# Where a ScalarE step of a weight conversion stands, the order of the second layer's products, and how far they trail, in an mLSTM, mixture-of-experts and MLP kernel on one core

## The chip, the cores and the metric

One core of a Trainium2 chip runs the whole program. Its engines work through instruction queues of their own, each in program order: TensorE (PE; its weight loads are shown apart as PEld), VectorE (DVE), ScalarE (ACT), GpSimd (POOL) and SyncE (SP), which only starts transfers here. The metric is the device time of one execution in microseconds (us), the median of several runs.

## The reference

Three stages follow each other. The middle one and the last matter here:

```python
x = attn_out.transpose(0, 2, 1, 3).reshape(B * S, H * D)   # mLSTM recurrence, 3072 tokens x 320
# mixture of experts: each token goes to the one expert (of 8) with the largest cosine
for e in range(E):
    mask = expert_idx == e
    h = np.maximum(x[mask] @ w1[e], 0.0)                    # 320 -> 1024
    out[mask] = gate_w[mask, None] * (h @ w2[e])            # 1024 -> 320
# gated MLP on all tokens
h = x @ w_in                                                # 320 -> 2048
g = h * (1.0 / (1.0 + np.exp(-1.702 * h)))
return (g @ w_out).astype(np.float32)                       # 2048 -> 320
```

The MLP's two weight arrays are float64; everything else is float32.

## The kernel before

**Stages.** The recurrence and the routing take the first part of the execution, and no edited line runs there. Then come 8 expert blocks (the loop over `steps`, 8 steps of 128 hidden units each), four of them 512 tokens wide, four 384. Then 7 MLP blocks, numbered 8 to 14, of 16 steps each: five 512 tokens wide, two 256.

**Split numbers.** Every float32 operand is kept as a high part and a remainder, so a product takes three matmuls: high by high, high by low, low by high. In a step, `h_mm` makes one PSUM tile `hp` from 8 matmuls (L138). Then the activation is split: for an expert, ACT makes the high part `hh` (L1093), and DVE the low part `hl` from it (L1094); for an MLP block the chain is `sg` on ACT (L1104), product on DVE (L1105), high part on ACT (L1106), low part on DVE (L1107). Then `o_mm` (L1120) adds three products for each of up to four 128-token row tiles into the PSUM tiles `acc`. In the last step of a block `o_mm` takes row tile after row tile with all three products (the `sorted` branch); in the others it makes all first products, then all second, then all with the low part.

**Trailing.** `o_mm` of a step stands in PE's queue after `h_mm` of a later step: one step later for the experts; for the MLP, two steps later in block 8 and in the two small blocks, one step later in blocks 9 to 12 (the list `left`). `put` and `put_out` copy `acc` to `o` after a block's last `o_mm`.

**Weights.** In each expert step ACT also casts the high parts of coming expert weights (L105, L118), and POOL (L110) and DVE (L111, L121) make their low parts. The float64 weights of the MLP are converted piece by piece meanwhile, 32 pieces, by the generator `cvt`: each `next` issues one stage of a piece, and `convert(n)` issues n stages at the end of a step (2 or 3 in wide blocks, 1 or 2 in narrow ones, 2 in block 8). First stage: ACT makes the fraction `fr` (L1160), DVE takes out the exponent `ex` (L1161), ACT turns it into `es` (L1163). The stages behind are DVE's: `mt` (L1165), `fr` (L1167), `es` (L1169, which reads ACT's `es`), `fr` (L1171). What is put on the list `late` is issued at the start of the next call of `convert`; before the change only the cast of a finished piece is put there.

The order in all queues is the order in which this code is written out (`manual_schedule`), and tile pools decide which buffer is reused.

Of the kernel before, what the change touches and what calls it, by code (L numbers as in the profile page):

```python
# [13 lines left out]
AF = mybir.ActivationFunctionType  # L14
# [6 lines left out]
CAP = 512  # L21
# [5 lines left out]
def kernel(ctx, tc, qT_in, kT_in, kvo_in, i_gate, f_gate, expert_emb, tau, w12, wio, out, dbg=None):  # L27

    nc = tc.nc
# [3 lines left out]
    E = expert_emb.shape[0]  # L33
# [972 lines left out]
    with ExitStack() as mctx:  # L1006
# [35 lines left out]
        ncol = lambda blk: GN if blk == "g" else COLS[blk]  # L1042
# [37 lines left out]
        def h_mm(blk, key, w, c0=0):  # L1080
            hp = ps_h.tile([P, CAP], F32, tag="hp", name="hp")
            nb = ncol(blk)
            hp_t[key] = hp[:, c0:nb]
            h_seq(hp_t[key], w, xh_t[blk][:, :, c0:nb], xl_t[blk][:, :, c0:nb])
# [12 lines left out]
        def swish_split(key):  # L1097
            hp = hp_t.pop(key)
            nb = hp.shape[-1]
            t = ring.tile([P, 2, CAP], F32, tag="w", name="sg")  # L1100
            sg, g = t[:, 0, 0:nb], t[:, 1, 0:nb]
            t = ring.tile([P, 2, CAP], F32R, tag="w", name="hhl")
            hh, hl = t[:, 0, 0:nb], t[:, 1, 0:nb]
            nc.scalar.activation(out=sg, in_=hp, func=AF.Sigmoid, scale=1.702)  # L1104
            nc.vector.tensor_tensor(out=g, in0=hp, in1=sg, op=ALU.mult)  # L1105
            nc.scalar.copy(hh, g)  # L1106
            nc.vector.tensor_tensor(out=hl, in0=g, in1=hh.bitcast(F32), op=ALU.subtract)  # L1107
            hs_t[key] = halves(hh, hl)

        def o_mm(blk, key, w, first, last):  # L1110
            hs = hs_t.pop(key)
            if first:
                acc_t[blk] = [ps_a.tile([P, DM], F32, tag="acc", name="acc") for _ in range(ncol(blk) // P)]


            n = ncol(blk) // P
            order_ = [(i, j) for j in range(3) for i in range(n)]
            for i, j in sorted(order_) if last else order_:
                hh, hl = hs[i]
                nc.tensor.matmul(acc_t[blk][i], hl if j == 2 else hh, w[:, DM:2 * DM] if j == 1 else w[:, 0:DM],  # L1120
                                 start=(first and j == 0), stop=(last and j == 2))
# [28 lines left out]
        exb = mp1.tile([P, 1], F32, name="exb")  # L1150

        def cvt(src, n, then):

            lo, hi = src[:, :, 0], src[:, :, 1]
            ex = mp2.tile([P, n], I32, tag="ex", name="ex", bufs=1)
            es = mp2.tile([P, n], I32, tag="sb", name="es", bufs=1)
            mt = mp2.tile([P, n], I32, tag="mt", name="mt", bufs=1)
            fr = mp2.tile([P, n], F32, tag="fr", name="fr")

            nc.scalar.activation(out=fr, in_=lo.bitcast(U32), func=AF.Copy, scale=2.0 ** -52, bias=1.0)  # L1160
            nc.vector.tensor_scalar(out=ex, in0=hi, scalar1=20, scalar2=0x7ff, op0=ALU.logical_shift_right, op1=ALU.bitwise_and)  # L1161

            nc.scalar.activation(out=es, in_=ex, func=AF.Relu, scale=float(2 ** 23), bias=exb)  # L1163
            yield
            nc.vector.tensor_scalar(out=mt, in0=hi, scalar1=0xfffff, scalar2=None, op0=ALU.bitwise_and)  # L1165
            yield
            nc.vector.scalar_tensor_tensor(out=fr, in0=mt, scalar=2.0 ** -20, in1=fr, op0=ALU.mult, op1=ALU.add)  # L1167
            yield
            nc.vector.scalar_tensor_tensor(out=es, in0=hi, scalar=-2147483648, in1=es, op0=ALU.bitwise_and, op1=ALU.bitwise_or)  # L1169
            yield  # L1170
            nc.vector.tensor_tensor(out=fr, in0=fr, in1=es.bitcast(F32), op=ALU.mult)  # L1171
            late.append(lambda: then(fr))
            yield

        craw, late = {}, []
# [6 lines left out]
        def cvt_all():  # L1182
            for m in range(M2):
                if 0 < m < M2 - 1:
                    load_c(m + 1)
                t = craw.pop(m)
                yield from cvt(t[:, 0:3 * P], 3 * P, lambda r, m=m: split_w1(win[:, m], r.rearrange("p (c f) -> p c f", c=3)))
                yield from cvt(t[:, 3 * P:], DM, lambda r, m=m: split_w2(wout[:, m], r))
# [49 lines left out]
        def load_y(blk):  # L1238
            n = ncol(blk)
            xg = xp.tile([P, NB, 3 * P], F32, tag="xr", name="xr", bufs=1)[:, 0:n // P]  # L1240
            src = y[row0(blk):row0(blk) + n, :].rearrange("(i p) d -> p i d", p=P)
            nc.sync.dma_start(out=xg[:, :, 0:DM], in_=src)
            nc.sync.dma_start(out=xg[:, :, DM:3 * P], in_=src[:, :, 2 * P:DM])
            xr_t[blk] = xg

        def scale_y(blk, eng=nc.gpsimd):
            n, t0 = ncol(blk) // P, row0(blk) // P
            eng.tensor_tensor(out=xr_t[blk], in0=xr_t[blk], in1=gated[:, t0:t0 + n].unsqueeze(2).to_broadcast([P, n, 3 * P]),  # L1248
                                    op=ALU.mult)
# [14 lines left out]
        def planes(blk, j, i):  # L1264

            if i == 0:
                xp_t[blk, j] = [half_tile(U16).rearrange("p (a i d) -> p a i d", a=2, d=3 * P),
                                half_tile(U16).rearrange("p (a c t) -> p a c t", a=2, t=GH)]
            pl, xT = xp_t[blk, j]
            nc.vector.tensor_copy(pl[:, :, i], xr_t[blk][:, j * GH // P + i].bitcast(U16).rearrange("p (d a) -> p a d", a=2))  # L1270
            for a in range(2):
                nc.sync.dma_start_transpose(out=xT[:, a, :, i * P:(i + 1) * P], in_=pl[:, a, i])

        def words(blk, j, a):

            if a == 0:
                xp_t[blk, j].append(half_tile(U16))
            pl, xT, t = xp_t[blk, j]
            nc.vector.tensor_copy(t.rearrange("p (n a) -> p a n", a=2)[:, a], xT[:, a].rearrange("p c t -> p (c t)"))

        def parts(blk, j, c):
            x = xp_t[blk, j][2].bitcast(F32).rearrange("p (c t) -> p c t", c=3)[:, c]
            if j == 0 and c == 0:
                xh_t[blk] = mp2.tile([P, 3, CAP], F32R, tag="xh", name="xh")
                xl_t[blk] = mp2.tile([P, 3, CAP], F32R, tag="xl", name="xl")
            js = slice(j * GH, (j + 1) * GH)
            nc.scalar.copy(xh_t[blk][:, c, js], x)  # L1287
            nc.vector.tensor_tensor(out=xl_t[blk][:, c, js], in0=x, in1=xh_t[blk][:, c, js].bitcast(F32), op=ALU.subtract)  # L1288
# [92 lines left out]
        with tc.manual_schedule():  # L1381
# [23 lines left out]
            def convert(n):  # L1405

                now, late[:] = late[:], []
                for f in now:
                    f()
                for _ in range(n):  # L1410
                    next(conv, None)

            def tail(p):
                e, m, s = p
                o_mm(e, ("a", s), wslot.pop(s)[1], m == 0, m == M1 - 1)
                if m == M1 - 1:
                    put(e)
# [55 lines left out]
            left = [prev]  # L1473
            for blk in range(E, len(COLS)):
                for m in range(M2):
                    h_mm(blk, ("b", blk, m), win[:, m])
                    swish_split(("b", blk, m))
                    left.append((blk, m))

                    while len(left) > (1 if E < blk and ncol(blk) == CAP else 2):  # L1480
                        p = left.pop(0)
                        (tail2 if len(p) == 2 else tail)(p)
                    if blk == E:
                        convert(2)
                    nxt = blk + 1
                    if nxt < len(COLS):
                        t = m - (2 if blk == E else 0)
                        small = ncol(blk) < CAP
                        if t == 2:
                            scale_y(nxt, nc.vector if small else nc.gpsimd)  # L1490
                        for j in range(ncol(nxt) // GH):
                            t0 = t - 3 * j
                            if 3 <= t0 < 5:
                                planes(nxt, j, t0 - 3)
                            w0 = t0 - (8 if small else 6)
                            if 0 <= w0 < 2:
                                words(nxt, j, w0)
                            if 2 <= w0 < 5:
                                parts(nxt, j, w0 - 2)
                        if t == 8 and nxt + 1 < len(COLS):  # L1500
                            load_y(nxt + 1)
# [68 lines left out]
```

## Time and profile before

| | |
|---|---|
| median of 3 runs | 806.28 us (805.17 to 807.76) |
| the profiled execution | 812.62 us, of which 810.9 us are the span |
| PE busy | 754.5 us (93%) |
| DVE busy | 566.7 us (70%) |
| ACT busy | 352.7 us (43%) |
| POOL busy | 250.9 us (31%) |

Times in the profile run from the first instruction. "Busy" is time in which an engine has at least one instruction in work; an idle gap in front of an instruction is given with the engine, operation and tile that ended it.

### The profile page before, as it was taken

To read this page: it belongs to the slowest core of one execution; us is meant where nothing else is said; L and a number is where in the kernel's file an instruction comes from. 1 tells how busy PE (TensorE), PEld (TensorE's weight loads), DVE (VectorE), ACT (ScalarE), POOL (GpSimd) and SP (SyncE) were. 2 spreads that over 40 slices of the span, in tenths; PEclk is the share of its full clock that TensorE was granted. 3 is DMA by queue.
4 is the path that set the end of the run, shared out by engine and by line. 5 is a ranking of instruction groups with operands and counts; after the bars stand their busy time and mean duration, and the time that the engine had idled before them with its cause. 6 is when DMAs were issued, how large, how long until landed. Compare 5 with 4: busy or idle time off the path is not lost.

```text
span 810.9 us, 13161 instructions
## 1 busy us (share of the span) xinstructions
PE 754.5 (93%) x4708; PEld 695.7 (86%) x4708; DVE 566.7 (70%) x1146; ACT 352.7 (43%) x834; POOL 250.9 (31%) x362
## 2 busy tenths in 40 slices
PE   6899898899799999999899999999999999999995
PEld 6899898898788788888889887888889898889995
DVE  8878888997498988888896777554454454445542
ACT  4352423324455555566564444333333343334442
POOL 5653567785132433345430100300300300201011
PEclk9788988989899999999999999999999999999998
DMA  7977866752636637557634212120120110200100
GB/s 207 321 240 248 270 204 217 243 188 94 210 117 200 224 110 236 146 176 198 194 106 144 90 20 59 38 53 20 46 66 1 53 40 1 71 1 17 38 17 16
DMA packets 70303, 100.20 MB, mean 124 GB/s; under 512 B 31120, under 2 KB 56472, under 8 KB 70232
## 3 DMA queue, kind: packets, MB, share of 16 engines
q1 hardware_dynamic: 67160, 91.41, 36.7%
q0 software_dynamic: 3072, 7.89, 2.6%
q8 instruction: 38, 0.62, 0.3%
q14 instruction: 33, 0.27, 0.1%
HBM read 77.53 MB, written 17.82 MB: 118 GB/s over the span
## 4 chain that ended last, share of the span: by engine, by line
issue 36%; DVE 12%; PE 5%; POOL 4%; ACT 4%; POOLq 0%; DVEq 0%; ACTq 0%
POOL out_dram L1142 3%; PE acc L1120 3%; PE hp L138 2%; DVE w L121 2%; DVE w L111 1%; POOL xr L1248 1%; DVE es L1169 1%; DVE fr L1167 1%; DVE hl L1094 1%; ACT hh L1093 1%; DVE sg L1105 1%; DVE ex L1161 1%; ACT hhl L1106 1%; DVE fr L1171 1%; DVE hhl L1107 1%
## 5 line engine op out<-in xcount | busy, mean ns | idle before, releaser
L1120 PE MATMUL acc<-wout,hhl 128*128 128x320 f32 x1152 | 187.8, 310 | 1.3 <-DVE hhl L1107 1.0
L1120 PEld LDWEIGHTS acc<-wout,hhl 128*128 128x128 f32 x1152 | 175.9, 188 | 9.6 <-DVE hhl L1107 1.2
L138 PE MATMUL hp<-xh,win 128*128 128x512 f32 (+1 forms) x560 | 131.5, 364 | 2.2 <-ACT xh L1287 1.5
L1105 DVE TENSOR_TENSOR sg<-hp,sg 128x512 f32<-128x512 f32 (+1 forms) x112 | 68.8, 614 | 88.5 <-ACT sg L1104 83.6
L1107 DVE TENSOR_TENSOR hhl<-sg,hhl 128x512 fp32r<-128x512 f32 (+1 forms) x112 | 73.4, 656 | 70.0 <-ACT hhl L1106 69.1
L1104 ACT ACTIVATE sg<-hp 128x512 f32<-128x512 f32 (+1 forms) x112 | 60.0, 536 | 113.2 <-PE hp L138 111.3
L1142 POOL DMA_INDIRECT out_dram<-o,tokd x24 | 23.7, 988 | 275.4 <-ACT o L1129 271.8
L138 PEld LDWEIGHTS hp<-xh,win 128*128 128x128 f32 x560 | 93.8, 188 | 14.5 <-ACT xh L1287 2.0
L1106 ACT CAST hhl<-sg 128x512 fp32r<-128x512 f32 (+1 forms) x112 | 62.6, 559 | 89.4 <-DVE sg L1105 85.8
L1120 PE MATMUL acc<-w,hh 128*128 128x320 f32 x424 | 81.0, 316 | 6.4 <-ACT hh L1093 5.2
L110 POOL TENSOR_TENSOR w<-r,w 128x256 fp32r<-128x256 f32 x58 | 45.8, 790 | 129.1 <-ACT w L105 126.6
L138 PE MATMUL hp<-xl,win 128*128 128x512 f32 (+1 forms) x336 | 85.7, 363 | 0.0
L1120 PEld LDWEIGHTS acc<-w,hh 128*128 128x128 f32 x424 | 67.2, 188 | 16.1 <-ACT hh L1093 10.6
L138 PE MATMUL hp<-xh,w 128*128 128x384 f32 (+2 forms) x320 | 75.8, 368 | 0.0
L138 PEld LDWEIGHTS hp<-xl,win 128*128 128x128 f32 x336 | 58.8, 189 | 11.0 <-DVE xl L1288 0.2
L400 PE MATMUL sp<-qT,kblk 120*128 120x128 f32 x384 | 58.1, 315 | 2.6 <-DVE wm L405 2.6
L360 DVE TENSOR_TENSOR_SCAN pm<-fb,ident_h 128x1024 f32<-128x1024 f32 x23 | 56.8, 2469 | 3.6 <-DMA fb<-dec 3.6
L138 PEld LDWEIGHTS hp<-xh,w 128*128 128x128 f32 x320 | 55.1, 193 | 3.7
L400 PEld LDWEIGHTS sp<-qT,kblk 120*128 120x128 f32 x384 | 54.6, 226 | 3.3 <-DVE wm L405 2.8
L1094 DVE SCALAR_TENSOR_TENSOR hl<-hp,hh 128x384 fp32r<-128x384 f32 (+2 forms) x64 | 38.1, 595 | 25.9 <-ACT hh L1093 25.9
L1120 PE MATMUL acc<-w,hl 128*128 128x320 f32 x212 | 46.5, 317 | 6.1 <-DVE hl L1094 5.9
L1163 ACT ACTIVATE es<-ex,exb 128x384 int32<-128x384 int32 (+1 forms) x32 | 18.9, 590 | 74.5 <-DVE ex L1161 74.5
(305 smaller groups left out, 1278.7 us busy)
## 6 DMA issues: line engine op xcount, KB each, us to landing
r<-in_w_dram SPq DMA_DIRECT2D x32, 704.0 KB
fb<-dec SPq DMA_DIRECT2D x23, 512.0 KB
kvo<-in_kvo_dram SPq DMA_DIRECT2D x24, 480.0 KB
c<-in_wio_dram SPq DMA_DIRECT2D x16, 704.0 KB
rows<-zt SPq DMA_DIRECT2D x8, 640.0 KB
qT<-in_qT_dram SPq DMA_DIRECT2D x24, 180.0 KB
xr<-y SPq DMA_DIRECT2D x5, 640.0 KB
kblk<-in_kT_dram SPq DMA_DIRECT2D x48, 60.0 KB
```

The lines of the kernel that those rows point to most:

```text
L110: eng.tensor_tensor(out=t[:, 3 * P:5 * P].rearrange("p (c f) -> p c f", c=2), in0=r1[:, 0:2], in1=hif[:, 0:2], op=ALU.subtract)
L138: nc.tensor.matmul(hp, a, b, start=(i == 0), stop=(i == len(seq) - 1))
L360: nc.vector.tensor_tensor_scan(out=pm[u].rearrange("p h t -> p (h t)"), data0=fb[u].rearrange("p h t -> p (h t)"), data1=ident_h.rearrange ...
L400: nc.tensor.matmul(sp[:, h - hs.start], kblk[u % NLD][0:KR, h // 3, h % 3, :], qT[u][0:KR, h // 3, :], start=True, stop=True)
L1094: nc.vector.scalar_tensor_tensor(out=hl, in0=hp, scalar=0.0, in1=hh.bitcast(F32), op0=ALU.max, op1=ALU.subtract)
L1104: nc.scalar.activation(out=sg, in_=hp, func=AF.Sigmoid, scale=1.702)
L1105: nc.vector.tensor_tensor(out=g, in0=hp, in1=sg, op=ALU.mult)
L1106: nc.scalar.copy(hh, g)
L1107: nc.vector.tensor_tensor(out=hl, in0=g, in1=hh.bitcast(F32), op=ALU.subtract)
L1120: nc.tensor.matmul(acc_t[blk][i], hl if j == 2 else hh, w[:, DM:2 * DM] if j == 1 else w[:, 0:DM], start=(first and j == 0), stop=(last an ...
L1142: sc = nc.gpsimd.indirect_dma_start(out=out, out_offset=bass.IndirectOffsetOnAxis(ap=tokd[:, ti:ti + 1], axis=0), in_=o[:, i], in_offset=None)
L1163: nc.scalar.activation(out=es, in_=ex, func=AF.Relu, scale=float(2 ** 23), bias=exb)
```

## The change

Three edits. ACT's `es` is put on the list `late`, so that it is issued at the start of the next step's `convert` and no longer right behind `fr`. In `o_mm`, outside a block's last step, the two products with the high part stand side by side for each row tile; those with the low part still come last. In blocks 9 to 12 `o_mm` trails by two steps, as in the other MLP blocks.

```diff
-            order_ = [(i, j) for j in range(3) for i in range(n)]
+            order_ = [(i, j) for i in range(n) for j in range(2)] + [(i, 2) for i in range(n)]
             for i, j in sorted(order_) if last else order_:
...
-            nc.scalar.activation(out=es, in_=ex, func=AF.Relu, scale=float(2 ** 23), bias=exb)
+            late.append(lambda: nc.scalar.activation(out=es, in_=ex, func=AF.Relu, scale=float(2 ** 23), bias=exb))
             yield
...
-                    while len(left) > (1 if E < blk and ncol(blk) == CAP else 2):
+                    while len(left) > 2:
```

ACT's queue in two steps of expert block 1, before (`hh` begins a step; `xh` is the coming block's input):

```order
L1093 ACTIVATE hh<-hp 128x512
L105 CAST w<-r 128x384
L118 CAST w<-r 128x320
L1160 ACTIVATE fr<-c 128x320
L1163 ACTIVATE es<-ex,exb 128x320
L1093 ACTIVATE hh<-hp 128x512
L105 CAST w<-r 128x384
L118 CAST w<-r 128x320
L1055 CAST xh<-xt 128x512
L105 CAST win<-fr 128x384
```

The same two steps after the change:

```order
L1093 ACTIVATE hh<-hp 128x512
L105 CAST w<-r 128x384
L118 CAST w<-r 128x320
L1160 ACTIVATE fr<-c 128x320
L1093 ACTIVATE hh<-hp 128x512
L105 CAST w<-r 128x384
L118 CAST w<-r 128x320
L1055 CAST xh<-xt 128x512
L105 CAST win<-fr 128x384
L1163 ACTIVATE es<-ex,exb 128x320
```

`es` has moved behind the next step's `hh`, its two or three casts and, where one is due, the cast of a finished piece. DVE's queue in the expert blocks is unchanged.

PE's queue where block 8 ends and block 9 has begun, before (`hhl` holds both parts of one step's activation, a number to a step; `acc` is numbered by row tile and block):

```order
L138 MATMUL hp_6370<-xh_6199,win_2407 128x512 x5
L138 MATMUL hp_6370<-xl_6200,win_2407 128x512 x3
...
L1120 MATMUL acc_5902<-wout_2408,hhl_6351 128x320 x3
L1120 MATMUL acc_5903<-wout_2408,hhl_6351 128x320 x3
L1120 MATMUL acc_5904<-wout_2408,hhl_6351 128x320 x3
L1120 MATMUL acc_5905<-wout_2408,hhl_6351 128x320 x3
L138 MATMUL hp_6422<-xh_6199,win_2407 128x512 x5
L138 MATMUL hp_6422<-xl_6200,win_2407 128x512 x3
L1120 MATMUL acc_6437<-wout_2408,hhl_6380 128x320
```

The left-out rows are the 12 products of block 8's last step but one. After the change:

```order
L138 MATMUL hp_6370<-xh_6199,win_2407 128x512 x5
L138 MATMUL hp_6370<-xl_6200,win_2407 128x512 x3
L1120 MATMUL acc_5901<-wout_2408,hhl_6320 128x320 x2
L1120 MATMUL acc_5902<-wout_2408,hhl_6320 128x320 x2
L1120 MATMUL acc_5903<-wout_2408,hhl_6320 128x320 x2
L1120 MATMUL acc_5904<-wout_2408,hhl_6320 128x320 x2
L1120 MATMUL acc_5901<-wout_2408,hhl_6320 128x320
...
L138 MATMUL hp_6397<-xh_6199,win_2407 128x512 x5
L138 MATMUL hp_6397<-xl_6200,win_2407 128x512 x3
L1120 MATMUL acc_5901<-wout_2408,hhl_6351 128x320 x3
```

Block 9's second `h_mm` now stands between the two last `o_mm` of block 8, and the products with the high part come in pairs on one `acc`. In the last step (three in a row on one `acc`) nothing has moved. POOL's and SP's queues are the same before and after.

## Rows read from the trace of the kernel before

**Rows 1.** Busy us (instructions) of PE, PEld, DVE, ACT, POOL by stretch; PE clock, DMA.

```profile
238.06:339.02 100.96, 96.03 (x515) 81.58 (x514) 86.71 (x170) 56.72 (x130) 35.97 (x54) 1.00 0.56 180
339.02:418.82 79.80, 73.11 (x440) 68.36 (x439) 70.46 (x138) 45.97 (x112) 34.83 (x53) 1.00 0.64 185
418.82:445.29 26.47, 24.07 (x151) 23.02 (x149) 18.93 (x41) 12.53 (x28) 3.57 (x5) 1.00 0.33 104
445.29:507.25 61.96, 59.41 (x315) 51.46 (x314) 45.79 (x84) 29.87 (x60) 5.15 (x4) 1.00 0.21 59
507.25:740.00 232.75, 231.80 (x1277) 208.19 (x1276) 115.52 (x183) 86.26 (x156) 26.55 (x36) 1.00 0.13 34
```

**Rows 2.** Timeline of PE, two successive steps of MLP block 9: start, us.

```profile
530.17 1.34 PE L138 MATMUL hp<-xh,win 128*128 128x512 f32 x5
...
533.81 1.34 PE L138 MATMUL hp<-xh,win 128*128 128x512 f32 x5
```

**Rows 3.** Timeline of PE, 384-wide expert steps, and four input transposes.

```profile
428.58 1.03 PE L138 MATMUL hp<-xh,w 128*128 128x384 f32 x5
...
431.29 1.05 PE L138 MATMUL hp<-xh,w 128*128 128x384 f32 x5
...
442.13 0.60 PE L1054 MATMUL xt<-ident,xr 128*128 128x128 f32 x4
442.49 1.12 PE L138 MATMUL hp<-xh,w 128*128 128x384 f32 x5
```

**Rows 4.** Waits from 238.06 to 418.82: total us, times, longest.

```profile
ACT es L1163 <- DVE ex L1161: 55.9, 22, 4.0
DVE hl L1094 <- ACT hh L1093: 18.7, 22, 1.2
...
PE acc L1120 <- DVE hl L1094: 5.9, 8, 1.5
...
PE acc L1120 <- ACT hh L1093: 4.4, 8, 1.1
```

**Rows 5.** Timeline of an expert step; in brackets the idle time before, and its releaser.

```profile
336.00 0.62 ACT L1163 ACTIVATE es<-ex,exb 128x384 int32<-128x384 int32 x1 [3.23 <-DVE ex L1161]
...
336.53 0.58 ACT L1093 ACTIVATE hh<-hp 128x512 fp32r<-128x512 f32 x1
...
337.13 0.69 DVE L1094 SCALAR_TENSOR_TENSOR hl<-hp,hh 128x512 fp32r<-128x512 f32 x1 [1.17 <-ACT hh L1093]
...
337.15 0.41 PE L1120 MATMUL acc<-w,hh 128*128 128x320 f32 x1 [0.45 <-ACT hh L1093]
```

**Rows 6.** Groups of instructions by line: busy us, mean ns of one.

```profile
L121 DVE TENSOR_TENSOR w<-r,w 128x320 fp32r<-128x320 f32 x64 | 35.5, 554 | 1.6
...
L1163 ACT ACTIVATE es<-ex,exb 128x384 int32<-128x384 int32 (+1 forms) x32 | 18.9, 590 | 74.5 <-DVE ex L1161 74.5
```

**Rows 7.** Timeline, last expert: the first MLP block's input is scaled and transposed.

```profile
433.91 1.76 DVE L1248 TENSOR_TENSOR xr<-xr,gated 128x1536 f32<-128x1536 f32 x1 [2.60 <-DMA xr<-y]
435.77 0.63 PE L1054 MATMUL xt<-ident,xr 128*128 128x128 f32 x4 [1.58 <-issue]
```

**Rows 8.** Waits from 445 to 507, MLP block 8.

```profile
ACT es L1163 <- DVE ex L1161: 8.4, 6, 3.4
...
PE hp L138 <- ACT xh L1287: 1.5, 1, 1.5
```

**Rows 9.** Timeline of PE, the last two `o_mm` of block 8.

```profile
507.25 3.68 PE L1120 MATMUL acc<-wout,hhl 128*128 128x320 f32 x24
510.77 1.34 PE L138 MATMUL hp<-xh,win 128*128 128x512 f32 x5
```

**Rows 10.** Timeline at the start of block 9.

```profile
514.92 3.60 DVE L1107 TENSOR_TENSOR hhl<-sg,hhl 128x512 fp32r<-128x512 f32 x1 [0.69 <-ACT hhl L1106]
...
515.21 2.75 POOL L1248 TENSOR_TENSOR xr<-xr,gated 128x1536 f32<-128x1536 f32 x1
...
516.28 1.34 PE L1120 MATMUL acc<-wout,hhl 128*128 128x320 f32 x8
...
518.57 0.42 PE L1120 MATMUL acc<-wout,hhl 128*128 128x320 f32 x1 [0.95 <-DVE hhl L1107]
```

## The prediction

> **What bounds the kernel now.** I read first the busy time by stretch [rows 1]. From 507 us to 740, blocks 9 to 12, PE is busy for 231.8 of 232.75 us: no edit can win much there. The three stretches from 238 to 445 us, expert blocks 1 to 7, are not like this: PE is idle in each while DVE is busy for 86, 88 and 72% of the time.
>
> How much PE loses there is read from its own pace. A wide step that waits for nothing takes 3.64 us from one `h_mm` to the next [rows 2], a narrow one 2.71, and four transposes 0.36 [rows 3]. A wide step has 8 matmuls of 512 columns and 12 of 320; the 24 products in a row of [rows 9] take 3.52 us, 0.147 each.
>
> - Experts 1 to 3: 24 x 3.64 + 33 transposes x 0.09 = 90.3 us of work, in 100.96 us: 10.6 lost.
> - Experts 4 to 6: 24 x 2.71 + 27 x 0.09 + three products more in the first step (0.44) = 67.9, in 79.80: 11.9 lost.
> - Expert 7: 8 x 2.71 + 12 x 0.09 = 22.8, in 26.47: 3.7 lost, of it some 1.8 (1.58 and a refill of the pipeline) at the transposes of [rows 7], for data that a transfer brings.
>
> Together 26 us. The waits say why [rows 4]: between 238 and 419 us ACT stands still 22 times, 55.9 us in all, in front of `es`, until DVE has made `ex`. Behind `es` in ACT's queue is the next step's `hh`. [rows 5] shows one turn of this: ACT idles 3.23 us for `ex`, makes `es`, and only then `hh`; DVE has nothing to do for 1.17 us until `hh` is there, and PE waits as well. DVE's idle time for `hh` sums to 18.7 us in 22 waits, as many as ACT has for `es`. So it is a ring: DVE is late, hence ACT, hence DVE again. PE's named waits, 4.4 us for `hh` and 5.9 for `hl`, are its outlet; each costs some 0.2 us more than the row says, since the end of a matmul is drawn behind its issue.
>
> **The change part by part.** *`es` one step later.* No instruction is added. The 32 `es` of 0.59 us [rows 6] are issued behind the next `hh` and its casts. `hh` then waits for PE alone. If DVE is late, ACT may still stop at `es`, but DVE has made `ex` before it begins the next step's `hl`, and what stands behind `es` is the `hh` after that, which DVE wants only when it has done a whole step's work. Hence the 18.7 us of DVE come back. What is late next is DVE's own work. Experts 1 to 3 need 86.7 us of DVE [rows 1], experts 4 to 6 need 70.5. Of DVE's idle time in the two stretches, 14.25 + 9.34 = 23.6 us, 4.9 are not waits for `hh`; I leave them, half to each. So DVE needs 89.2 and 72.9 us, PE 90.3 and 67.9. The longer ones are 90.3 and 72.9, together 163.2 against 180.8 now: 17.6 us at most.
>
> Two engines so close to full don't mesh without loss, though `hl` may be late by most of a step before PE feels it. No row shows the friction, so it is bounded: nothing (17.6 us won) to half (8.8). I take a quarter, 13.2 won, because wide steps between two stalls already run at PE's pace here and there.
>
> In expert 7 DVE has room (18.9 of 26.47 us). 3.7 less the 1.8 of the transfer leaves 1.9; I take 1.5, with bounds 0.5 and 3: an earlier write-out could shorten the transfer's wait too.
>
> In block 8 the same ACT wait comes 6 times, 8.4 us [rows 8]. PE's one long wait there, 1.5 us, is for the last part of block 9's input, which ACT and DVE finish late. If they are less late, up to 2.5 us return (with shorter waits of PE and refills); none does if the chain of that input itself sets its time. I take 1.5.
>
> A new wait is possible: DVE's `es` (L1169) reads ACT's. Where both would come first behind the casts, ACT needs 0.59 us for `es` behind L118, and DVE in the same time 0.55 for L121 [rows 6]. In the worst step ACT has two more casts, but DVE has their partner subtractions too. Queued behind L1169 is the next `hl`, for which PE waits at last. Bounds 0 and 0.3 us for each of 22; the friction covers it.
>
> *Products in pairs.* In the last steps three products follow on one `acc` today, in the others never; [rows 9] holds both kinds, 12 and 12, in 3.52 us, so neither is slower: 0.147 each. The low-part products stay last, so `hl` is not wanted earlier. At the start of a block the second `acc` is wanted 0.15 us later, the fourth 0.45 later, which can help where a copy-out is late. Value 0, bounds 0 and 1 us won over the blocks; a loss has no place in that row.
>
> *Blocks 9 to 12 two steps behind.* The work stays. At the start of block 9 POOL scales for 2.75 us, and beside it DVE's subtraction takes 3.60 [rows 10], where one of the same width took 0.69 [rows 5]. PE, one step behind, needs the result and goes on at 518.57 and not at 516.28 + 8 x 0.147 = 517.46: 1.1 us. With a step more in between, 3.64 us, this is covered. In the rest of blocks 9 to 12 PE is full, so nothing is to be won. The copy-out of a block, its four scatters and so POOL's scaling come one step later; the next input's first copy on DVE stands a step behind them, and PE now has that step of slack too. Cost 0, at most some 1 us per block start, three of them. So 1.1 won, bounds 1.1 won and 2 lost.
>
> [...]
>
> **Sum.** 13.2 + 1.5 + 1.5 + 0 + 1.1 = 17.3 us. The profiled execution took 812.62 us, so it would take 795.3. The median before is 806.28, 6.3 us less than the profiled one; the part that changes is idle time of the same stages, so I take the same difference: 789.0 us.
>
> **The rivals.**
>
> *Only the named waits go.* DVE may stay as late as it is, with its freed time lost again to its own order or to waits for PE. Then only PE's waits for `hh` vanish: 4.4 us and 8 refills of 0.2, 6.0; with 1.1 from block 9 and 1 from expert 7 it is 8 us, 798. For it: the largest waits for `hl` come in last steps of a block, where `hl` is wanted at once. Against it: DVE's idle time for `hh` would have to be replaced by another.
>
> *The wait moves to DVE (slower).* If L1169 waits for ACT's `es` at its new place, DVE loses in its own queue what it won at `hl`. The point at which it turns is 18.7 / 22 = 0.85 us per piece. At 1.5 us per piece, the 22 pieces cost 33 us and return 18.7; DVE, nearly full, passes most of the 14 on to PE, in part covered by its slack of a step: about 6 us lost, 812. For it: `es` now stands behind up to four casts. Against: those casts have DVE partners, and ACT is busy for only 57% of these stretches.
>
> *POOL's collisions eat the gain.* POOL is busy for 36.0 + 34.8 of 180.8 us in experts 1 to 6 [rows 1], and DVE's subtraction beside POOL took five times its usual 0.69 us [rows 10]. If a tighter beat puts POOL's low parts on DVE's work every time, a quarter of those 70.8 us, 17.7, would come on top, as much as is to be won: 806, no change. Against it: ACT's cast starts POOL's and DVE's low parts together today already, so much of it is in the 86.7 and 70.5. [...]
>
> **How the numbers follow.** My own case, `hh` is free and friction takes up to half of 17.6: from 8.8 + 0.5 + 0 + 0 = 9.3 won to 17.6 + 3 + 2.5 + 1 + 1.1, some 25 with everything at its best, which I cut to 22: 784 to 797, chance 0.64. Only the named waits: 796 to 802, 0.18. POOL eats it, or something else that I don't see cancels it: 0.10. The wait moves: 0.08. A measurement of this kernel tells about 0.3%, 2.4 us, from no change, so faster means below 803.9: 0.64 + 0.18 = 0.82; same 0.10; slower 0.08. The range takes in the first two cases and a little at either end: 783 to 804.
>
> **What the profile will show.** If I am right, ACT's waits for `ex` fall from 55.9 us to a few, DVE's waits for `hh` to under 5, and the stretch of experts 1 to 6 takes some 167 us; PE's remaining waits are for `hl`. L1169 then has no waits for ACT beyond 0.3 us each. At the start of block 9 the slow subtraction is there still, and PE goes past it. The pitch of 3.64 us stays. I am wrong if DVE idles for ACT's `es`, if DVE's busy time in experts 1 to 6 grows beyond 157 us by more than a few, or if a wait for `acc` or for the next block's input appears in blocks 9 to 12.

## The result and the profile after

The changed kernel takes 782.36 us (median of 4 runs, 779.7 to 787.84), the kernel before, run beside it, 807.02 (805.17 to 811.71). The ratio is 0.9695, interval 0.9627 to 0.9762: 3% faster, 24.7 us. Forecast were 17.3 us; the time lies 0.6 us below the range. In a second series the changed kernel took 784.51 (783.21 to 786.15) against 810.97, ratio 0.9672 (0.9639 to 0.9704).

The profiled execution took 781.83 us, of them 780.1 span. PE is busy for 734.6 us (94%), DVE 558.0 (72%), ACT 356.3 (46%), POOL 250.3 (32%).

The stretches of [rows 1] after the change, cut at the same `h_mm` for the first three (columns as there). The last two rows are block 8 and blocks 9 to 13. The row of block 8 holds one step more than in [rows 1] (20 matmuls, 3.64 us), since a step of block 9 now stands inside it; without it block 8 takes 58.5 us against 61.96:

```profile
232.23:324.60 92.37, 91.07 (x515) 81.96 (x514) 85.24 (x175) 58.00 (x130) 36.72 (x55) 1.00 0.66 205
324.60:393.37 68.77, 68.77 (x440) 68.46 (x439) 65.65 (x133) 47.57 (x112) 35.66 (x51) 1.00 0.77 204
393.37:419.19 25.82, 23.55 (x151) 23.04 (x150) 19.09 (x43) 12.88 (x29) 3.28 (x4) 1.00 0.38 107
419.19:481.30 62.11, 62.04 (x335) 54.70 (x334) 46.21 (x85) 30.51 (x60) 5.17 (x4) 1.00 0.21 58
481.30:740.00 258.70, 258.70 (x1493) 235.74 (x1492) 130.85 (x224) 100.01 (x192) 31.50 (x44) 1.00 0.13 35
```

Experts 1 to 3 went from 100.96 to 92.37 us, experts 4 to 6 from 79.80 to 68.77, expert 7 from 26.47 to 25.82, the MLP to the end from 365.61 to 360.91. Expert 0 (not among the rows), from its first `h_mm` on, went from 26.09 to 24.95. Together 26.1 us. Of the 1.1 us of expert 0 only 0.3 are the change's: its last step takes 3.95 us before (3.93 to 3.97 in the other profiles with `es` at its old place and POOL's subtractions there), and 3.63 in both profiles of the changed kernel and with `es` alone. The other 0.8 lie in its second step, which ran at a granted clock of 0.69 before and 0.88 here, but at 0.67 in the second profile of the changed kernel (4.04 us for 3.95 before). The part ahead of expert 0, in which no edited line runs, was 4.7 us shorter here, at a clock of 0.92 against 0.87, but it varied between 205 and 213 us in the profiles of all kernels; it is no part of the change either. In experts 4 to 6 PE is now busy in every microsecond.

DVE's column holds a surprise: in experts 1 to 6 its busy time fell from 157.2 to 150.9 us, with the same 308 instructions (five of them now fall ahead of the cut between the two rows).

The waits of the same two stretches, which answer to [rows 4]:

```profile
POOL w L110 <- ACT w L105: 82.1, 44, 5.0
ACT hh L1093 <- PE hp L138: 35.3, 37, 1.8
ACT es L1163 <- DVE ex L1161: 3.6, 4, 1.8
DVE hl L1094 <- ACT hh L1093: 3.1, 7, 0.8
PE acc L1120 <- DVE hl L1094: 1.3, 1, 1.3
```

ACT's waits for `ex` went from 55.9 us to 3.6, DVE's for `hh` from 18.7 to 3.1, and PE's for `hh` are gone. `hh` now waits for PE, 37 times: ACT is ahead, and PE sets the beat. DVE's `es` (L1169) has no wait for ACT at all.

The start of block 9, which answers to [rows 10], in the timelines of DVE, POOL and PE:

```profile
489.49 0.69 DVE L1105 TENSOR_TENSOR sg<-hp,sg 128x512 f32<-128x512 f32 x1 [1.57 <-ACT sg L1104]
490.87 1.46 DVE L1107 TENSOR_TENSOR hhl<-sg,hhl 128x512 fp32r<-128x512 f32 x1 [0.69 <-ACT hhl L1106]
...
493.13 0.69 DVE L1105 TENSOR_TENSOR sg<-hp,sg 128x512 f32<-128x512 f32 x1 [0.33 <-ACT sg L1104]
494.50 0.69 DVE L1107 TENSOR_TENSOR hhl<-sg,hhl 128x512 fp32r<-128x512 f32 x1 [0.69 <-ACT hhl L1106]
...
489.02 2.75 POOL L1248 TENSOR_TENSOR xr<-xr,gated 128x1536 f32<-128x1536 f32 x1
...
490.36 1.34 PE L138 MATMUL hp<-xh,win 128*128 128x512 f32 x5
...
494.00 1.34 PE L138 MATMUL hp<-xh,win 128*128 128x512 f32 x5
```

The subtraction is still slow beside POOL (1.46 us here for 0.69 alone), and PE goes past it at its pitch of 3.64 us, as the step more of trailing lets it.

### The profile page after: what moved, and what is told of

Same layout as the page of the kernel before. It is cut to its first block, busy times and chain, and to the rows that moved or that the text cites. A ratio compares the mean times of both kernels' runs of the same rounds, so it can differ in the third digit from the quotient of the medians.

```text
span 780.1 us, 13253 instructions
## 1 busy us (share of the span) xinstructions
PE 734.6 (94%) x4708; PEld 687.3 (88%) x4708; DVE 558.0 (72%) x1146; ACT 356.3 (46%) x834; POOL 250.3 (32%) x362
## 4 chain that ended last, share of the span: by engine, by line
issue 37%; PE 22%; DVE 8%; POOL 5%; ACT 1%; POOLq 0%; DVEq 0%; ACTq 0%
PE hp L138 11%; PE acc L1120 10%; POOL out_dram L1142 3%; POOL xr L1248 1%; DVE w L121 1%; PE xt L1054 1%; ACT hhl L1106 1%; DVE sg L1105 1%; DVE ex L1161 1%; DVE hhl L1107 1%; DVE hl L1094 1%; DVE es L1169 1%; DVE fr L1171 1%; DVE w L111 1%; DVE xl L1056 0%
## 5 line engine op out<-in xcount | busy, mean ns | idle before, releaser
L1107 DVE TENSOR_TENSOR hhl<-sg,hhl 128x512 fp32r<-128x512 f32 (+1 forms) x112 | 71.3, 637 | 70.0 <-ACT hhl L1106 70.0
L110 POOL TENSOR_TENSOR w<-r,w 128x256 fp32r<-128x256 f32 x58 | 46.5, 801 | 108.8 <-ACT w L105 108.4
L1120 PE MATMUL acc<-w,hh 128*128 128x320 f32 x424 | 75.6, 309 | 0.0
L400 PE MATMUL sp<-qT,kblk 120*128 120x128 f32 x384 | 54.7, 302 | 3.1 <-DVE wm L405 3.1
L400 PEld LDWEIGHTS sp<-qT,kblk 120*128 120x128 f32 x384 | 51.5, 216 | 3.7 <-DVE wm L405 3.3
L1093 ACT ACTIVATE hh<-hp 128x384 fp32r<-128x384 f32 (+2 forms) x64 | 33.5, 524 | 44.4 <-PE hp L138 43.3
L138 PE MATMUL hp<-xl,w 128*128 128x384 f32 (+2 forms) x192 | 47.8, 358 | 0.0
L1120 PE MATMUL acc<-w,hl 128*128 128x320 f32 x212 | 44.9, 310 | 1.4 <-DVE hl L1094 1.3
```

The costliest lines, as they stand in the source:

```text
L110: eng.tensor_tensor(out=t[:, 3 * P:5 * P].rearrange("p (c f) -> p c f", c=2), in0=r1[:, 0:2], in1=hif[:, 0:2], op=ALU.subtract)
L138: nc.tensor.matmul(hp, a, b, start=(i == 0), stop=(i == len(seq) - 1))
L400: nc.tensor.matmul(sp[:, h - hs.start], kblk[u % NLD][0:KR, h // 3, h % 3, :], qT[u][0:KR, h // 3, :], start=True, stop=True)
L1093: nc.scalar.activation(out=hh, in_=hp, func=AF.Relu)
```

## The experiments

The table gives, from each kernel's profile, the length of the stretches (us), and DVE's busy time in experts 1 to 6; "median" and "ratio" are of timed runs, the ratio against the kernel before in the same series. The kernel before had medians from 807.0 to 812.3 us in the five series, so medians of different series can't be set against each other, and the ratios can.

| kernel | experts 1–6 | DVE busy there | expert 7 | MLP | median | ratio (interval) |
|---|---|---|---|---|---|---|
| before | 180.8 | 157.2 | 26.5 | 365.6 | 807.02 | |
| changed | 161.1 | 150.9 | 25.8 | 360.9 | 782.36 | 0.9695 (0.9627 to 0.9762) |
| `es` alone | 161.2 | 151.0 | 25.5 | 362.6 | 787.76 | 0.9683 (0.9641 to 0.9726) |
| pairs alone | 180.8 | 157.2 | 26.5 | 365.6 | 811.55 | 1.0002 (0.9972 to 1.0032) |
| trailing alone | 180.7 | 157.1 | 28.5 | 364.4 | 811.33 | 0.9990 (0.9954 to 1.0026) |
| all but `es` | 180.8 | 157.2 | 26.9 | 364.4 | 810.12 | 0.9975 (0.9942 to 1.0008) |
| `es` ahead of the casts | 167.5 | 155.2 | 27.6 | 361.0 | 792.81 | 0.9766 (0.9733 to 0.9800) |
| more work for DVE | 174.9 | 167.9 | 28.4 | 364.2 | 802.27 | 0.9895 (0.9861 to 0.9928) |
| before, no POOL low parts | 159.9 | 132.2 | 23.0 | 365.4 | 787.22 | 0.9749 (0.9694 to 0.9804) |
| changed, no POOL low parts | 159.3 | 133.6 | 23.1 | 365.4 | 784.23 | 0.9714 (0.9672 to 0.9755) |
| before, no `mt` | 176.9 | 150.5 | 26.7 | 364.7 | 804.26 | 0.9937 (0.9909 to 0.9964) |
| changed, earlier load of y | 161.2 | 151.0 | 23.5 | 360.9 | 779.18 | 0.9608 (0.9570 to 0.9646) |

### Which edit carries it

Each edit alone, put into the kernel before, and the two small ones together. The first alone:

```diff
-            nc.scalar.activation(out=es, in_=ex, func=AF.Relu, scale=float(2 ** 23), bias=exb)
+            late.append(lambda: nc.scalar.activation(out=es, in_=ex, func=AF.Relu, scale=float(2 ** 23), bias=exb))
```

> The first edit alone; the other two are as before. Theory (hh no longer stands behind es, so the ring of DVE and ACT in the expert blocks is broken): nearly the whole gain, 780 to 788 us, and PE's waits in experts 1 to 6 as short as after the full change. Rival (the three edits share the gain, the pairs of products or the second step of trailing giving many microseconds): 790 to 800 us.

> The products in pairs alone. Theory: no matmul gets faster and hl comes last as before, so the time stays within 2.4 us of before, 804 to 809 us, and PE's waits for hh and hl in the expert blocks stay near 10 us. Rival (acc wanted later at the start of a block is worth much): 798 to 803 us.

> Blocks 9 to 12 two steps behind, alone. Theory: only the 1.1 us at the start of block 9 goes, 804 to 808 us. Rival (more waits in the MLP go, since the profile after the full change shows some 4.7 us less there): 801 to 803 us.

> The second and third edit together, es where it was before. Theory: 803 to 807 us, the ring of waits between ACT and DVE is there in full (some 56 us of ACT's waits for ex in experts 1 to 6). Rival (the edits help each other or carry much of the gain themselves): under 800 us.

Windows of the kernel with the first edit alone (experts 1 to 3, 4 to 6, 7), and then of the one with the pairs alone:

```profile
237.76:330.19 92.43, 91.06 (x516) 81.97 (x515) 85.31 (x175) 58.04 (x130) 36.82 (x55) 1.00 0.67 204
330.19:398.99 68.80, 68.80 (x441) 68.48 (x439) 65.69 (x133) 47.57 (x112) 35.67 (x51) 1.00 0.77 205
398.99:424.49 25.50, 23.54 (x151) 23.03 (x149) 19.11 (x43) 12.88 (x29) 3.28 (x4) 1.00 0.36 108
```

```profile
233.09:334.13 101.04, 95.71 (x515) 81.16 (x514) 86.79 (x170) 56.65 (x130) 35.87 (x54) 1.00 0.57 180
334.13:413.91 79.78, 72.71 (x441) 68.22 (x440) 70.44 (x138) 45.95 (x112) 34.66 (x53) 1.00 0.64 185
```

The first edit by itself has all of the gain in the experts, and 3.0 of the MLP's 4.7 us. These 3.0 lie in block 8: the step in which block 9's input was awaited takes 5.45 us and not 7.24, four other steps (3.73 to 4.20 before, from one `h_mm` to the next) are back at the pitch. Pairs alone change no stretch by more than 0.1 us; what they win at the start of block 8, where a copy-out is late (a step of 4.27 us and not 4.69), the next step loses again, waiting for `sg`. With `es` moved that loss doesn't follow: the step takes 4.19 us in the changed kernel and 4.62 with `es` alone, so the pairs are worth 0.4 us there. Trailing alone takes 1.2 us off the MLP, which is too little for its timed interval to tell from nothing; its expert 7 ran at a granted clock of 0.94, and the extra 2 us there are in no kernel that had `es` at its old place and the clock at full. The 27.6 and 28.4 us of two kernels below were at 0.94 as well.

### Where `es` has to stand

In the changed kernel `es` stands behind the next `hh` and the casts. Here it is put right behind `hh`, ahead of the casts:

```diff
-            late.append(lambda: nc.scalar.activation(out=es, in_=ex, func=AF.Relu, scale=float(2 ** 23), bias=exb))
+            es_late.append(lambda: nc.scalar.activation(out=es, in_=ex, func=AF.Relu, scale=float(2 ** 23), bias=exb))
...
+                    flush_es()
```

> The change, but es right behind the next step's hh, ahead of that step's casts. Theory (all that counts is that hh no longer stands behind es): within 3 us of the changed kernel; DVE, which needs the casts behind es, waits a little for them. Rival (es must be so late that ex is long done when ACT comes to it, or ACT's stall is given back through the casts): ACT still waits for ex tens of microseconds in all and 8 us or more of the gain are lost.

Its waits in experts 1 to 6:

```profile
ACT es L1163 <- DVE ex L1161: 30.0, 22, 2.3
ACT hh L1093 <- PE hp L138: 17.6, 24, 1.8
...
DVE w L111 <- ACT w L105: 7.3, 18, 0.9
```

8.3 us slower than the changed kernel of the same series, so the rival held; in the profiles 6.3 us of it are in experts 1 to 6, and 1.8 to 2.7 in expert 7, which ran at the lower clock. ACT again stands at `es` for each of the 22 pieces, and now the casts behind it are late, and DVE waits for those: the ring is closed again, over `w` in place of `hh`. So it is not enough that `hh` is ahead of `es`: of what DVE takes from ACT in that step, the casts count as well. Places between the casts were not run.

### How near DVE is to the bound

In the changed kernel `mt` is done three times in each piece, which adds 44 instructions in experts 1 to 6:

```diff
+            for _ in range(2):
+                nc.vector.tensor_scalar(out=mt, in0=hi, scalar1=0xfffff, scalar2=None, op0=ALU.bitwise_and)
```

> The change, with DVE's stage mt done three times instead of once in each of the 32 pieces: 64 instructions of some 0.34 us more, 22 us of work for DVE and nothing else. The prediction's term (DVE is as full as PE in experts 1 to 6): DVE has 7 us to spare in experts 1 to 3 and 3 us in 4 to 6, and needs 9 and 6 more, so those stretches grow by 5 us or more, and block 8 by some more. Rival (DVE's busy time is elastic, much of it being collisions with POOL that fall away or are hidden): within 2 us of the changed kernel.

```profile
233.42:331.89 98.47, 94.59 (x515) 83.41 (x514) 94.01 (x197) 58.67 (x131) 37.80 (x56) 0.98 0.59 179
331.89:408.35 76.46, 71.51 (x441) 68.71 (x439) 73.84 (x155) 46.65 (x112) 35.59 (x51) 1.00 0.71 201
```

DVE's busy time in these two windows grew by 17.0 us, the stretches by 13.8, as the prediction's term said. A small part of it passed at a lower granted clock (0.98 in experts 1 to 3): the second step of expert 1 took 4.25 us in place of 3.63. With `es` moved, DVE stands right behind PE; most of what is given to it shows in the time.

### What makes DVE late: GpSimd's low parts

In the kernel before, POOL's subtraction (L110) is replaced by a fill with zeros; the same is done in the changed kernel.

```diff
+        if eng is nc.gpsimd:
+            eng.memset(t[:, 3 * P:5 * P].bitcast(F32), 0.0)
+        else:
```

> The kernel before, with POOL's subtraction that makes the low part of the first-layer weights replaced by a fill with zeros (it leaves out that correction of the product): hardly any of POOL's work beside DVE is left in the expert blocks. Theory (the ring of waits itself holds PE back, whatever makes DVE late first): ACT's waits for ex in the expert blocks stay above 35 us and the gain stays under 10 us of the 24. Rival (collisions of DVE with POOL are what makes DVE late, and the ring only passes it on): 15 us or more faster than before.

> The same replacement in the changed kernel. Theory (PE is at its own pace in the expert blocks already): within 2 us of the changed kernel, though DVE's busy time in experts 1 to 6 falls by 10 us or more. Rival (collisions still cost PE time): 5 us or more faster than the changed kernel.

Windows (experts 1 to 3, 4 to 6) and waits of the kernel before without these subtractions; line numbers are 3 higher in it:

```profile
232.96:324.40 91.44, 91.37 (x515) 82.00 (x514) 75.46 (x169) 58.08 (x131) 22.47 (x55) 1.00 0.68 204
324.40:392.90 68.50, 68.50 (x440) 68.45 (x439) 56.69 (x138) 47.25 (x113) 19.18 (x48) 1.00 0.77 209
```

```profile
ACT es L1166 <- DVE ex L1164: 26.5, 23, 3.0
ACT hh L1096 <- PE hp L141: 23.2, 23, 1.7
DVE hl L1097 <- ACT hh L1096: 20.3, 26, 1.2
```

`es` stands at its old place, the ring's waits are there (DVE's for `hh` even 1.6 us longer than in [rows 4]), and yet PE runs at its pace. The theory failed and the rival held: ACT's waits for `ex` are 26.5 us, not above 35, and the run is 23.1 us shorter. What has gone is 25.0 us of DVE's busy time. Its groups by line show where, first in the kernel before, then without POOL's subtractions (busy us, mean ns of one, then the idle time before):

```profile
L1094 DVE SCALAR_TENSOR_TENSOR hl<-hp,hh 128x512 fp32r<-128x512 f32 (+1 forms) x48 | 29.9, 622 | 18.7 <-ACT hh L1093 18.7
...
L111 DVE TENSOR_TENSOR w<-r,w 64x128 fp32r<-64x128 f32 x49 | 23.7, 485 | 1.6
L1167 DVE SCALAR_TENSOR_TENSOR fr<-mt,fr 128x320 f32<-128x320 int32 (+1 forms) x22 | 15.5, 705 | 1.0
...
L1165 DVE TENSOR_SCALAR mt<-c 128x320 int32<-128x320 int32 (+1 forms) x22 | 11.8, 538 | 0.1
```

```profile
L1097 DVE SCALAR_TENSOR_TENSOR hl<-hp,hh 128x512 fp32r<-128x512 f32 (+1 forms) x49 | 30.6, 624 | 20.7 <-ACT hh L1096 20.3
...
L114 DVE TENSOR_TENSOR w<-r,w 64x128 fp32r<-64x128 f32 x48 | 13.9, 290 | 2.4 <-ACT w L105 0.9
...
L1170 DVE SCALAR_TENSOR_TENSOR fr<-mt,fr 128x320 f32<-128x320 int32 (+1 forms) x22 | 11.5, 523 | 0.8
...
L1168 DVE TENSOR_SCALAR mt<-c 128x320 int32<-128x320 int32 (+1 forms) x23 | 8.3, 360 | 0.1
```

A 64x128 low part takes 290 ns and not 485, `mt` 360 and not 538, while `hl`, which reads PSUM, takes the same (622 and 624). One collision in the timelines of the kernel before, DVE and POOL:

```profile
248.22 1.17 DVE L1165 TENSOR_SCALAR mt<-c 128x384 int32<-128x384 int32 x1
249.49 0.56 DVE L1167 SCALAR_TENSOR_TENSOR fr<-mt,fr 128x384 f32<-128x384 int32 x1
...
248.40 0.75 POOL L110 TENSOR_TENSOR w<-r,w 128x256 fp32r<-128x256 f32 x1
```

`mt` of this shape takes 0.35 us where POOL has no work beside it; here it ends 0.24 us behind POOL's subtraction. In experts 1 to 6 of this kernel `mt` met POOL's subtraction in 7 of 22 places and took 0.75 to 1.17 us there, 0.32 to 0.36 in the others.

Windows of the changed kernel without POOL's subtractions (experts 1 to 3, 4 to 6):

```profile
230.74:321.54 90.80, 90.80 (x515) 81.96 (x514) 75.53 (x169) 57.16 (x128) 22.93 (x55) 1.00 0.68 204
321.54:390.05 68.51, 68.51 (x441) 68.47 (x439) 58.03 (x137) 47.32 (x113) 19.52 (x48) 1.00 0.78 209
```

In the changed kernel, taking POOL's subtractions out saves only 1.8 us in experts 1 to 6 and 2 to 3 in expert 7, while the MLP takes 4.5 more (3.1 of them are one wait of PE for a copy-out on ACT at the start of block 8); so both kernels without them are near one another. The two causes don't add: either one taken away brings the experts to PE's pace.

### Less work for DVE, the ring left in place

In the kernel before, `mt` is left out.

```diff
-            nc.vector.tensor_scalar(out=mt, in0=hi, scalar1=0xfffff, scalar2=None, op0=ALU.bitwise_and)
...
-            nc.vector.scalar_tensor_tensor(out=fr, in0=mt, scalar=2.0 ** -20, in1=fr, op0=ALU.mult, op1=ALU.add)
+            nc.vector.scalar_tensor_tensor(out=fr, in0=hi, scalar=2.0 ** -20, in1=fr, op0=ALU.mult, op1=ALU.add)
```

> The kernel before, with VectorE's instruction mt left out and fr reading hi directly, so that the fraction of the weights converted on VectorE is wrong; the waits between ScalarE and VectorE stay as they are. It takes about 11.8 us of VectorE's work out of experts 1 to 6 (22 instructions of 0.54). Theory (VectorE's whole time, its work, its collisions with GpSimd and its turn of the ring, is the limit in the kernel before): experts 1 to 6 fall from 180.8 to 168 to 172 and the run is 9 to 14 us shorter. Rival (the ring alone sets the pace, whatever VectorE has to do): experts 1 to 6 stay within 3 us of 180.8, and the run within 5 us of the kernel before.

The one wait of DVE in experts 1 to 6, and in the timelines of DVE and POOL the place of the collision above:

```profile
DVE hl L1094 <- ACT hh L1093: 22.5, 22, 1.2
```

```profile
245.42 1.36 DVE L1165 SCALAR_TENSOR_TENSOR fr<-c,fr 128x384 f32<-128x384 int32 x1
246.71 0.68 DVE L1094 SCALAR_TENSOR_TENSOR hl<-hp,hh 128x512 fp32r<-128x512 f32 x1
...
245.60 0.76 POOL L110 TENSOR_TENSOR w<-r,w 128x256 fp32r<-128x256 f32 x1
```

11.8 us of instructions are gone, and experts 1 to 6 are only 3.9 us shorter: between what the theory and the rival expected, nearer the rival. The other 7.9 went two ways. DVE's busy time fell by 6.7 and not by 11.8: the collision stays and moves to the next instruction, here `fr` with 1.36 us (its mean rose from 705 to 858 ns, 3.4 us in all; it is L1165 in this kernel). And DVE waits 3.8 us more for `hh`; its other idle time is 1.0 us less. Of the 22 turns of the ring in the kernel before, DVE had nothing between `ex` and the next `hl` in 10, and waited 11.0 us in these, 1.1 each; in 12 it had `mt` there (in 4 `fr` too) and waited 7.7. Without `mt` 18 have nothing, and wait 19.7 us, again 1.1 each. So the ring costs DVE 1.1 us a turn (ACT's `es` of 0.59 and `hh` of 0.58), less the work that happens to stand in the gap; taking out work that stands there makes the gap longer and not the turn shorter.

### A version that is faster than both

Expert 7 still waits for the transfer of y. It is started earlier:

```diff
+                if e == E - 2 and m == 5:
+                    load_y(E)
...
-                    if m == 1:
-                        load_y(E)
```

> The change, and the first MLP block's input is loaded one expert earlier, ahead of the write-out of expert 6, whose rows it doesn't need. Theory (the last long wait of PE, some 2.1 us at the transposes in expert 7, is for that write-out): 1.5 to 2.5 us less than the changed kernel. Rival (that wait only moves to the next thing that comes late, or the earlier transfer disturbs others): no difference within 1 us.

Expert 7 in the changed kernel, two of its waits, and the window of expert 7 with the earlier load:

```profile
DVE xr L1248 <- DMA xr<-y: 3.2, 1, 3.2
...
PE xt L1054 <- issue: 2.1, 1, 2.1
```

```profile
394.79:418.29 23.50, 23.36 (x151) 23.07 (x149) 19.02 (x43) 12.88 (x29) 3.29 (x4) 1.00 0.32 85
```

In the changed kernel SP holds the load back 4.5 us until the write-out of expert 6 is done; here it starts the load 12 us ahead of that write-out. Both waits are gone, and expert 7 takes 23.50 us against 25.82 and 24.93 in the two profiles of the changed kernel. The median is 779.18 us against 784.51 of the same series; 1.4 to 2.3 of these 5.3 us are the stretch's, the rest lies within what the part ahead of the experts varies by. The intervals of the two ratios just overlap (0.9570 to 0.9646, and 0.9639 to 0.9704 for the changed kernel in that series), so it is the stretch, not the median, that shows the gain.

## Why the prediction fell short

The direction, the place and the mechanism were right: the ring of ACT and DVE over `es` and `hh` was opened, its waits went as said, L1169 waits for nothing, and PE's pitch stayed. The size was too small by 7.4 us, and these are terms of the sum. The step that failed most is DVE's floor in experts 1 to 6, which took its busy time as fixed; beside it failed the friction set on top of that floor.

- **Experts 1 to 6: 13.2 forecast, 19.6 measured.** Two steps of this term failed. *The floors*: "DVE needs 89.2 and 72.9 us" took DVE's busy time as fixed, so that experts 4 to 6 were to stay 5 us above PE's work of 67.9; they took 68.77, 4.1 less than the floor. DVE's busy time isn't fixed: it holds what POOL's subtractions cost DVE, 25.0 us in the kernel before and 17.3 in the changed one (150.9 less 133.6, each against its own twin without POOL's subtractions), and some of it went with the new order. By line `mt` fell most, from 538 ns to 338, about its time without POOL's subtractions (360), while `ex` rose from 359 to 483. *The friction* of a quarter, 4.4 us: experts 1 to 3 took 2.1 us more than their floor of 90.3. The rest of the miss is here, 2.3. Against PE's own 158.2 us the two stretches lost 2.9, and one wait for `hl` of 1.3 is all that PE shows there. In DVE's terms the 19.6 us are 15.6 of its waits for `hh` and 6.3 of its busy time, less 2.3 more of other idle time: of the 18.7 of waits that were to come back most did, and the 6.3 were put at nothing. The line of `ex` before (that of `mt` is shown above), then both in the changed kernel:

```profile
L1161 DVE TENSOR_SCALAR ex<-c 128x320 int32<-128x320 int32 (+1 forms) x22 | 7.9, 359 | 0.1
...
L1161 DVE TENSOR_SCALAR ex<-c 128x320 int32<-128x320 int32 (+1 forms) x22 | 10.6, 483 | 0.1
L1165 DVE TENSOR_SCALAR mt<-c 128x320 int32<-128x320 int32 (+1 forms) x22 | 7.4, 338 | 0.1
```

A step of slack for `hl` was enough for DVE at 94% and PE at 99% busy.

- **Expert 0: nothing forecast, 0.3 measured**, though pieces are converted there as well; the same edit, left out of the sum. The 0.8 us more between the two profiles are the clock's.
- **Expert 7: 1.5 forecast, 0.65 and 1.5 in the two profiles.** The transfer's wait stayed, as the sum had it.
- **Block 8: 1.5 forecast, 3.0 measured** with `es` alone. The whole wait for block 9's input went, with its refill (1.79 us of that step, for a wait of 1.53), and four steps of 0.1 to 0.6 us over the pitch, which the waits of [rows 8] don't name.
- **Pairs: 0 forecast**, 0 alone and 0.4 beside `es`, within the bounds; **trailing: 1.1 forecast, 1.2 measured.** No wait for `acc` or for the next input appeared.

The rivals: "only the named waits go" would have left 798 us. "The wait moves to DVE" didn't come about behind the casts; ahead of the casts a wait of this kind did, for `w`, and cost 6.3 us of the gain in experts 1 to 6, not all of it. "POOL's collisions eat the gain" had the right thing in view with the wrong sign: collisions made up 25.0 of DVE's 157.2 busy us, and in the changed kernel they make up 17.3. The 17.7 us that it set on top, a quarter of POOL's 70.8, were the author's estimate and no run shows them: DVE's busy time fell by 6.3.

Which of DVE's instructions POOL's subtractions make longer is read by line, in the kernel before and in its twin without them (mean ns of one): the 64x128 low part `w`, with two inputs in SBUF, 485 and 290; `mt`, a `tensor_scalar` with one input, in SBUF, 538 and 360; `hl`, `xl` and the copy-out, which read PSUM, 622 and 624, 593 and 598, 480 and 483. `ex`, a `tensor_scalar` as well, took 1.46 us at 301.02 in the changed kernel, beside two of POOL's subtractions, and 0.32 to 0.36 in 17 of its 22 places.

**What stays open.** DVE's busy time (157.2 us), its waits for `hh` (18.7) and its other idle time (4.9) fill the 180.8 us of the kernel before, but the run without `mt` shows that these terms feed one another, so such a sum doesn't forecast an edit by itself. That POOL's subtractions cost DVE less in the new order is shown; why they do, which start of which engine decides it, stays open: no run here changed POOL's start alone.

## What to carry to other kernels

Where two engines wait for each other in turn, look in the queue of the one for what stands behind its waiting instruction, and put all that the other engine wants in that step ahead of it, not the first piece alone. An engine's busy time is no floor where its instructions take longer beside another engine's, as `mt` did here (1.17 us for 0.35): take the duration of an instruction where nothing stands beside it, and count the rest as something that an order can give back, here 7.7 of 25.0 us. Work is worth taking out only where it doesn't stand in a gap that would be waited through anyway.

## What the runs showed of the hardware that was not expected

DVE's instructions that read PSUM weren't slowed by POOL here: the product of 0.69 us at 489.49 ran inside a POOL operation of 2.75, as at 493.13, where POOL has no work (0.69), while the subtraction on SBUF behind it took 1.46. The instruction that is slowed may be one that began first by the records: `mt` began 0.18 us ahead of POOL's subtraction and ended 0.24 behind it, and the subtraction at 514.92 in [rows 10] began 0.29 ahead of POOL's scaling; POOL's spans are rough, so the order of the two within the engines isn't known from this. The ends are more regular: the slowed instruction ends behind POOL's by its own time less some 0.12 us, `mt` by 0.24 (0.35 alone) and the subtraction by 0.56 (0.69 alone), at 514.92 as at 490.87. In these rows the end follows that of POOL's operation and not the time spent beside it: the subtraction had all 2.75 us of the scaling beside it at 514.92, and 0.90 at 490.87.
